# Interleaved block products, adds straight from PSUM, spread weight sums and another DMA order in a fused attention and mixture-of-experts kernel

## The chip, the cores and the metric

The kernel runs on one core of a Trainium2 chip. The metric is the device time of one execution, in microseconds (us), lower is better. Times are medians of several runs; the profile is of one execution.

## The reference

```python
def reference(q, k, v, w_gate, w1, w2):          # q, k, v: 4 x 8 heads x 576 x 64
    scores = q @ k.T / 8                          # per head
    scores = where(0 <= i - j < 64, scores, -1e9) # window of 64
    x = (softmax(scores) @ v)                     # x: 2304 tokens x 512
    P = exp(x @ w_gate - max)                     # 2304 x 8
    for _ in range(8):                            # Sinkhorn
        P /= P.sum(1) + 1e-9
        P /= P.sum(0) + 1e-9
        P *= 2304 / 8
    out = 0
    for e in range(8):                            # w1[e]: 512 x 1024, w2[e]: 1024 x 512
        out += P[:, e:e+1] * (relu(x @ w1[e]) @ w2[e])
    return out                                    # float32, 2304 x 512
```

## The kernel before, in words

Every float32 matrix product is done as three products of rounded parts: each operand is split into a high part (a cast to fp32r) and a low part (the operand minus its high part), and high*high, high*low and low*high are added in PSUM. Most products also go by a seven-product scheme on 2x2 blocks (Strassen-Winograd): a product needs sums of blocks of its operands, and its seven products are added up in three PSUM accumulators, a, b and c (tags qa, qb, qc, two buffers each).

The 18 tiles of 128 tokens are worked on in three passes of six tiles. The program has three stages.

Stage 1 is attention for all 18 tiles, on TensorE, with the first half of expert 0 for them. The tiles of passes 1 and 2 write their x to DRAM (`xd_r`), and the block sums of x, four operations of GpSimd for each pair of tiles (`x_sums`, L293 to L300), are written to `xd_t`. The rows of expert 0's first half go to `yd`.

Stage 2 is pass 0. It has 15 units (u = 0 to 14) of two groups; a group is 256 of the 1024 hidden columns of an expert. `Group.run` (L225) does the seven products of a group (`product`, L203; the matmuls are L209, 128x384 each, six for a product), with ScalarE copies that seed a bank with another (L229, L232, L234), ScalarE relu (L214) and VectorE low parts (L219) and adds (L222). Its hooks `extra(0)` to `extra(3)` issue side work: `even(k)` in the first group, `odd(k)` in the second. Then `mm2` (L257) does six output tiles, each twelve matmuls 128x512 (L268) into a PSUM tile yp, of which there are two buffers, and one VectorE operation that scales and adds it to `acc` (L287; expert 0: L275). Beside this the weights of the next groups are fetched (`fetch1`, `fetch2`: L121, L128), summed on GpSimd for w1 (`sums1`, L138 to L141), split into high and low on ScalarE and GpSimd (`split1`: L156, L158; `split2`: L171, L172), and kept in DRAM for the later passes (`keep1`: w1d, L163). For w2 the four block sums are VectorE's (`sums2`, L182 to L185); they are written to a tile tf, of which there is one, and `keep2` (L191) writes it to w2d. `sums2(s+2)` stands at the end of the first group and `sums2(s+3)` at the end of the second.

Stage 3 is passes 1 and 2. `first(p, i)` (from L875 on) does the seven products of a group i with the kept w1 (L209 again) and makes seven high and low tiles G of its relu (L886, L889, and `part_s` L892 on ScalarE, L893 on GpSimd, for the four block sums sm made at L896 and L924). `second(p, u, o)` (L927 on) does, for a pair o of token tiles, seven products with the two groups of unit u (L940, 128x256, six for a product), four scaled adds to `acc` (`out_add`, L947), two ScalarE copies (p5 L956, u2 L958), the seed copy L953 and two VectorE adds (L963, L966). `split_w2` (L867 on ScalarE, L868 on GpSimd) splits the kept w2 blocks, from a queue `bulk` that is worked off a piece at a time. The order is first(0), first(1), first(2), unit 0, first(3), first(4), unit 1 and so on, where a unit is second for o = 0, 1, 2; each second and each first is issued whole. At a pass's end the finished rows of `acc` go out, and those of the next pass's `yd` come in, in turn (L289 and L290; L993 and L995), and `load_x` reads the next x and its sums.

The order on each engine is the order in which the program is written (manual scheduling), and all DMAs are issued by SyncE in program order; a DMA that has to wait holds up those behind it.

Of the kernel before, what the change touches and what calls it, by code (L numbers as in the profile page):

```python
# [21 lines left out]
def window_attention_sinkhorn_moe(ctx: ExitStack, tc: tile.TileContext, q, k, v, w_gate, w1, w2, out):  # L22
# [46 lines left out]
    xd_t = [dram.tile([P, 4, 2, NB], F32, name=f"xd_t{p}") for p in range(1, NPASS)]  # L69
# [30 lines left out]
    r_tf = Ring("tf", [P, 4, 2 * P], F32, 0, 1)  # L100
# [23 lines left out]
    def fetch2(i):  # L124
        if i < len(groups):
            e, c = groups[i]
# [48 lines left out]
    tsum = {}  # L175

    def sums2(i):
        if i >= len(groups):
            return
        a, t = raw2.pop(i), r_tf.new()  # L180
# [5 lines left out]
        tsum[i] = t  # L186

    def keep2(i):
        if i < len(groups):
            u, g = divmod(i, 2)  # L190
            nc.sync.dma_start(out=w2d[u][:, :, g], in_=tsum.pop(i))  # L191
# [65 lines left out]
    def mm2(u, t):  # L257
# [60 lines left out]
    with tc.manual_schedule():  # L318
        with ExitStack() as p1:
            at_p = p1.enter_context(tc.tile_pool(name="at", bufs=2))  # L320
            ps_h = p1.enter_context(tc.tile_pool(name="ps_h", bufs=3, space=PSUM))
# [28 lines left out]
            def load_qkv(t, names="kqv"):  # L350
                for nm in names:
                    src = {"k": k, "q": q, "v": v}[nm]
                    x = at_p.tile([P, H, D], F32, tag=nm, name=nm, bufs=3 if nm == "v" else 2)
# [13 lines left out]
            def new_kT(t):  # L367
                kT[t] = at_p.tile([P, G, WIN + P], F32, tag="kT", name="kT")
# [102 lines left out]
            def x_parts(j):  # L471
# [4 lines left out]
                for slot, k0, c0 in ((0, 0, 0), (1, 2, 0), (2, 2, P)):  # L476
                    dst = f32(xc[slot]) if pp == 0 else xd_r[pp - 1][:, slot]
                    for a in range(2):
                        nc.sync.dma_start(out=dst[:, a, :, cols], in_=f32(x[:, a, k0:k0 + 2, c0:c0 + P]))
                xt = at_p.tile([P, 4, 2, P], F32, tag="xt", name="xt", bufs=1)  # L480
                x_sums(xt, xr[j], nc.gpsimd)
                if pp:
                    nc.sync.dma_start(out=xd_t[pp - 1][:, :, :, cols], in_=xt)
                    return
# [89 lines left out]
            for nm, src in (("k", k), ("q", q)):  # L574
                raw[nm, 0] = at_p.tile([P, H, D], F32, tag=nm, name=nm, bufs=2)
# [106 lines left out]
        def load_x(p, xt):  # L682

# [368 lines left out]
```

## Time and profile before

| | us |
|---|---|
| median of three runs | 1776.28 |
| lowest and highest | 1768.73 and 1780.81 |
| the profiled execution | 1783.53 |
| its span, first to last instruction | 1781.8 |
| TensorE busy | 1640.1 (92% of the span) |
| GpSimd, VectorE, ScalarE busy | 1002.6, 947.0, 825.2 |
| mean granted TensorE clock | 0.951 |

PE is TensorE (PEld its weight loads), DVE VectorE, ACT ScalarE, POOL GpSimd, SP SyncE. A row of a timeline has start, duration, engine, line, operation, output<-inputs, shapes, how many instructions follow each other (x6), and in brackets how long the engine stood idle before, and for whom. The chain of waits lists start, duration and what was running, followed back from the end. A row of the stretches has length, then busy time and instructions of PE, PEld, DVE, ACT and POOL, the granted clock (1.00 is full), the DMA share and GB/s.

### The profile page before, as it was taken

The page shows a single profiled execution, that of the slowest core. Times are in us where ns is not written, and L with a number is a line of the kernel's source. Part 1 is how long each engine was busy: PE and PEld are TensorE (multiplying, and loading weights), DVE is VectorE, ACT ScalarE, POOL GpSimd, SP SyncE. Part 2 cuts the span into 40 slices and gives each one's busy share as a digit, 9 for nine tenths or more (in the row PEclk, how much of TensorE's full clock was granted, in tenths as well). Part 3 has the DMA queues.
Part 4 walks back from the last instruction along what each step waited for, and adds up shares of the span by engine and source line. Part 5 has one row for each costly group of instructions (what it writes and reads, how often), then busy time and mean ns, then how long its engine had stood idle before and what let it go on. Part 6 is the DMA issues. An engine that isn't in the chain of part 4 may idle for free.

```text
span 1781.8 us, 29339 instructions
## 1 busy us (share of the span) xinstructions
PE 1640.1 (92%) x10875; PEld 1531.1 (86%) x10875; DVE 947.0 (53%) x1742; ACT 825.2 (46%) x1856; POOL 1002.6 (56%) x924
## 2 busy tenths in 40 slices
PE   7999967889989999895899999999979999999998
PEld 6778766778877888785899999999969999999998
DVE  6456446665554445543455555565535555555554
ACT  5556432333332233323455555555534555555553
POOL 6234445645565455615565656565646566665654
PEclk9899988999998999998899999999988999999999
DMA  8675655564445544465555555555763555555551
GB/s 196 145 163 126 169 178 177 204 232 156 177 154 207 221 162 159 161 271 185 176 172 180 185 180 184 182 185 167 259 218 132 164 203 166 206 160 193 177 177 60
DMA packets 210831, 319.26 MB, mean 179 GB/s; under 512 B 68416, under 2 KB 143168, under 8 KB 206848
## 3 DMA queue, kind: packets, MB, share of 16 engines
q1 hardware_dynamic: 210688, 317.39, 54.1%
q8 instruction: 85, 1.39, 0.3%
q14 instruction: 58, 0.48, 0.1%
HBM read 223.89 MB, written 86.51 MB: 174 GB/s over the span
## 4 chain that ended last, share of the span: by engine, by line
PE 62%; DVE 10%; DMA 7%; ACT 2%; POOL 2%; issue 1%; SPq 1%; DVEq 0%; POOLq 0%; ACTq 0%
PE qb L940 12%; PE qb L209 11%; PE yp L268 11%; PE qa L209 8%; PE qc L209 8%; PE qc L940 6%; PE qa L940 6%; DMA w2d<-tf 4%; DVE tf L183 2%; DVE g L219 2%; DMA out_dram<-acc 2%; DVE tf L184 1%; DVE tf L182 1%; ACT g L214 1%; DVE sm L896 1%
## 5 line engine op out<-in xcount | busy, mean ns | idle before, releaser
L868 POOL TENSOR_TENSOR wp<-wr,wp 128x512 fp32r<-128x512 f32 x210 | 279.3, 1342 | 135.5 <-ACT wp L867 86.5
L209 PE MATMUL qb<-xc,w1c 128*128 128x384 f32 x1620 | 329.4, 339 | 14.5 <-ACT qb L229 5.4
L268 PE MATMUL yp<-w2c,g 128*128 128x512 f32 x1080 | 284.5, 425 | 59.1 <-DVE acc L287 37.8
L268 PEld LDWEIGHTS yp<-w2c,g 128*128 128x128 f32 x1080 | 223.2, 209 | 113.4 <-DVE acc L287 42.4
L209 PEld LDWEIGHTS qb<-xc,w1c 128*128 128x128 f32 x1620 | 287.9, 190 | 15.7 <-ACT qb L229 5.8
L940 PE MATMUL qb<-wp,G 128*128 128x256 f32 x1620 | 255.3, 294 | 25.5 <-ACT qb L953 12.8
L940 PEld LDWEIGHTS qb<-wp,G 128*128 128x128 f32 x1620 | 211.7, 191 | 39.7 <-ACT qb L953 21.5
L893 POOL TENSOR_TENSOR G<-sm,G 128x384 fp32r<-128x384 f32 x240 | 241.4, 1040 | 0.0
L209 PE MATMUL qa<-xc,w1c 128*128 128x384 f32 x1080 | 220.5, 340 | 10.2 <-DMA w1c<-w1d 10.2
L209 PE MATMUL qc<-xc,w1c 128*128 128x384 f32 x1080 | 218.2, 337 | 0.0
L924 POOL TENSOR_TENSOR sm<-sm,r 128x384 f32<-128x384 f32 x60 | 61.1, 1018 | 268.3 <-DVE sm L896 206.4
L172 POOL TENSOR_TENSOR w2c<-stg,w2c 128x512 fp32r<-128x512 f32 x60 | 86.0, 1454 | 212.3 <-PE qb L209 202.3
L209 PEld LDWEIGHTS qa<-xc,w1c 128*128 128x128 f32 x1080 | 192.1, 190 | 11.6 <-DMA w1c<-w1d 10.5
L209 PEld LDWEIGHTS qc<-xc,w1c 128*128 128x128 f32 x1080 | 191.7, 189 | 0.0
L940 PE MATMUL qc<-wp,G 128*128 128x256 f32 x1080 | 160.3, 284 | 3.9 <-POOL G L893 3.5
L940 PE MATMUL qa<-wp,G 128*128 128x256 f32 x1080 | 160.4, 285 | 0.0
L222 DVE TENSOR_TENSOR c<-qb,p 128x384 f32<-128x384 f32 x60 | 33.5, 558 | 223.6 <-PE qb L209 223.6
L867 ACT CAST wp<-wr 128x512 fp32r<-128x512 f32 x210 | 127.6, 622 | 49.5 <-DMA wr<-in_moe_w_dram 35.4
L940 PEld LDWEIGHTS qc<-wp,G 128*128 128x128 f32 x1080 | 143.8, 193 | 4.7 <-POOL G L893 3.9
L940 PEld LDWEIGHTS qa<-wp,G 128*128 128x128 f32 x1080 | 146.0, 193 | 0.0
L892 ACT CAST G<-sm 128x384 fp32r<-128x384 f32 x240 | 120.0, 513 | 55.3 <-DVE sm L896 49.1
L947 DVE SCALAR_TENSOR_TENSOR acc<-qa,prob,acc 128x256 f32<-128x256 f32 x90 | 43.6, 484 | 145.0 <-PE qa L940 145.0
(166 smaller groups left out, 2350.0 us busy)
## 6 DMA issues: line engine op xcount, KB each, us to landing
w1c<-w1d SPq DMA_DIRECT2D x180, 512.0 KB, 5.5
w1d<-w1c SPq DMA_DIRECT2D x30, 1792.0 KB, 11.0
stg<-in_moe_w_dram SPq DMA_DIRECT2D x62, 512.0 KB, 5.3
wr<-w2d SPq DMA_DIRECT2D x120, 256.0 KB, 3.0
wr<-in_moe_w_dram SPq DMA_DIRECT2D x90, 256.0 KB, 2.8
w2d<-tf SPq DMA_DIRECT2D x30, 512.0 KB, 5.1
w1c<-w1d SPq DMA_DIRECT2D x60, 256.0 KB, 2.8
xd_r<-xs SPq DMA_DIRECT2D x36, 128.0 KB, 2.5
```

Source lines behind the costliest of these rows:

```text
L172: nc.gpsimd.tensor_tensor(out=w[:, 1], in0=src[:, j], in1=f32(w[:, 0]), op=ALU.subtract)
L183: nc.vector.tensor_tensor(out=t[:, 1], in0=t[:, 0], in1=b22, op=ALU.subtract)
L209: nc.tensor.matmul(bank, lhsT=w[:, ws, a, kk, :], rhs=xc[xs][:, b, kk, :], start=(first and j == 0), stop=(j == 5), skip_group_check=not f ...
L219: nc.vector.scalar_tensor_tensor(out=g[:, 1, :], in0=src, scalar=0.0, in1=f32(g[:, 0, :]), op0=ALU.max, op1=ALU.subtract)
L268: nc.tensor.matmul(yp, lhsT=g[:, a, o:o + P], rhs=w[:, x, :], start=(i == 0), stop=(i == 11))
L867: nc.scalar.copy(out=t[:, :, 0, :], in_=r)
L868: nc.gpsimd.tensor_tensor(out=t[:, :, 1, :], in0=r, in1=f32(t[:, :, 0, :]), op=ALU.subtract)
L892: nc.scalar.copy(out=g[:, 3 + k, 0, :], in_=sm[k])
L893: nc.gpsimd.tensor_tensor(out=g[:, 3 + k, 1, :], in0=sm[k], in1=f32(g[:, 3 + k, 0, :]), op=ALU.subtract)
L924: nc.gpsimd.tensor_tensor(out=sm[2], in0=sm[1], in1=r22, op=ALU.add)
L940: nc.tensor.matmul(bank, lhsT=G7[p, 2 * u + g][:, gp, x, cols], rhs=W[p, u, wp][:, g, y, :], start=(start and j == 0), stop=(j == 5), skip ...
L947: nc.vector.scalar_tensor_tensor(out=at, in0=src, scalar=prob[:, t0 + row, e:e + 1], in1=at, op0=ALU.mult, op1=ALU.add)
```

## The change

What it does, part by part:

1. **w2 sums in stage 2.** tf has two buffers. `sums2` puts its four operations into a list `t_ops`, and `sum_step` issues one of them behind each output tile of `mm2`, one more at the start of each group of the next unit. The sums are those of the groups s+4 and s+5 (before: s+2 and s+3); those of the first four groups are done in the last two units, from four further fetches.
2. **x sums of passes 1 and 2.** Attention writes the raw x to DRAM (`xd_f`). `next_sums` reads it back in stage 2 and does the 24 GpSimd operations there, in units 4 to 6 (pass 2) and 9 to 11 (pass 1). Pass 1's stay in SBUF, so `load_x(1)` reads three blocks rather than seven.
3. **Pools.** The attention tiles of q, k and kT lie at the other side of SBUF, so other tiles are under the ones of stage 2.
4. **Row DMAs.** The in-turn pair L289 and L290 is gone. All six output rows are issued together behind the first three w2 loads of stage 3, and the six loads of `acc` in the first group. At the end of pass 1 they are split likewise. `load_x(2)` is issued earlier, its high and low parts are made inside the last unit.
5. **Stage 3.** `first` and `second` become classes with `step(n)`, one product each. Neighbours are interleaved: each block issues 6, 2, [1 of the next block], 7, 3, [5 of the next block], 4. In `Second` the copies p5 and u2 and the two adds are gone: six `out_add` read PSUM directly. The scaling of `acc` by the first gate column is moved from GpSimd (L980) to VectorE.

The core of the diff:

```diff
-    r_tf = Ring("tf", [P, 4, 2 * P], F32, 0, 1)
+    r_tf = Ring("tf", [P, 4, 2 * P], F32, 0, 2)
...
     def sums2(i):
-        nc.vector.tensor_tensor(out=t[:, 0], in0=b12, in1=b11, op=ALU.subtract)
-        nc.vector.tensor_tensor(out=t[:, 1], in0=t[:, 0], in1=b22, op=ALU.subtract)
-        nc.vector.tensor_tensor(out=t[:, 2], in0=b22, in1=b12, op=ALU.subtract)
-        nc.vector.tensor_tensor(out=t[:, 3], in0=b21, in1=t[:, 1], op=ALU.add)
+        for k, x, y, op in ((0, b12, b11, ALU.subtract), (2, b22, b12, ALU.subtract), (1, t[:, 0], b22, ALU.subtract), (3, b21, t[:, 1], ALU.add)):
+            t_ops.append(lambda k=k, x=x, y=y, op=op: nc.vector.tensor_tensor(out=t[:, k], in0=x, in1=y, op=op))
...
-        if e == E - 1 and not first:
-            nc.sync.dma_start(out=out[tt * P:(tt + 1) * P, :], in_=at)
-            nc.sync.dma_start(out=at, in_=yd[FIRST[1] + t])
...
+                if pp:
+                    nc.sync.dma_start(out=xd_f[pp - 1][jj], in_=xr[j])
+                    return
                 xt = at_p.tile([P, 4, 2, P], F32, tag="xt", name="xt", bufs=1)
                 x_sums(xt, xr[j], nc.gpsimd)
-                if pp:
-                    nc.sync.dma_start(out=xd_t[pp - 1][:, :, :, cols], in_=xt)
-                    return
...
                 for t in range(TP):
+                    if t == 0:
+                        sums2(s + 4)
+                        sums2(s + 5)
                     mm2(u, t)
+                    sum_step(2 if last and t > 3 else 1)
...
-                product(1, a, True)
-                nc.scalar.copy(out=b, in_=a)
-                do_bulk(1)
-                product(5, c, True)
-                nc.scalar.copy(out=p5, in_=c)
-                product(6, b, False)
-                nc.scalar.copy(out=u2, in_=b)
-                do_bulk(2)
-                product(2, a, False)
-                out_add(1, 0, a)
-                product(7, b, False)
-                nc.vector.tensor_tensor(out=c22, in0=b, in1=p5, op=ALU.add)
-                out_add(0, 1, c22)
-                product(3, c, False)
-                nc.vector.tensor_tensor(out=c, in0=c, in1=u2, op=ALU.add)
-                out_add(1, 1, c)
-                product(4, b, False)
-                out_add(0, 0, b)
+                    elif n == 5:
+                        self.product(5, self.c, True)
+                        self.out_add(0, 1, self.c)
+                    elif n == 6:
+                        self.product(6, self.b, False)
+                        self.out_add(1, 1, self.b)
+                    elif n == 2:
+                        self.product(2, self.a, False)
+                        self.out_add(1, 0, self.a)
+                    elif n == 7:
+                        self.product(7, self.b, False)
+                        self.out_add(0, 1, self.b)
+                    elif n == 3:
+                        self.product(3, self.c, False)
+                        self.out_add(1, 1, self.c)
+                    else:
+                        self.product(4, self.b, False)
+                        self.out_add(0, 0, self.b)
...
+            for _ in range(3):
+                load_w2()
+            queue_w2((1, 0), range(7))
+            out_rows(0, range(TP))
...
+                hook(F[0], 6, lambda p=p: acc_rows(p))
...
+                for k, blk in enumerate(flow):
+                    nx = flow[k + 1] if k + 1 < len(flow) else None
+                    for st in (6, 2, -1, 7, 3, -5, 4):
+                        if st > 0:
+                            go(blk, st)
+                        elif nx:
+                            go(nx, -st)
```

Three places show how it moves the instructions. (A number behind a name tells one tile from the next of its kind.)

First, VectorE in stage 2, from the last product of a unit's second group into its output tiles. Before, tf is the one tile of the w2 sums and stg the fetched weights:

```order
L219 SCALAR_TENSOR_TENSOR g_5_5432<-qb,g_5_5432 128x384
L182 TENSOR_TENSOR tf_5436<-stg_5181 128x256
L183 TENSOR_TENSOR tf_5436<-tf_5436,stg_5181 128x256
L184 TENSOR_TENSOR tf_5436<-stg_5181 128x256
L185 TENSOR_TENSOR tf_5436<-stg_5181,tf_5436 128x256
L287 SCALAR_TENSOR_TENSOR acc<-yp_5455,prob,acc 128x512
L287 SCALAR_TENSOR_TENSOR acc<-yp_5470,prob,acc 128x512
```

and now:

```order
L222 SCALAR_TENSOR_TENSOR g_5_5413<-qb,g_5_5413 128x384
L290 SCALAR_TENSOR_TENSOR acc<-yp_5433,prob,acc 128x512
L184 TENSOR_TENSOR tf_5431<-stg_5385 128x256
L290 SCALAR_TENSOR_TENSOR acc<-yp_5448,prob,acc 128x512
L184 TENSOR_TENSOR tf_5431<-stg_5385 128x256
L290 SCALAR_TENSOR_TENSOR acc<-yp_5463,prob,acc 128x512
L184 TENSOR_TENSOR tf_5431<-tf_5431,stg_5385 128x256
```

The four sums that stood ahead of the first add of an output tile now stand singly behind the adds.

Second, the DMA issues of SyncE at the start of stage 3. Before (wr is a w2 block of stage 3, yd the rows for the next pass):

```order
L290 DMA acc<-yd_100 128x512
L289 DMA out_dram<-acc 128x512
L290 DMA acc<-yd_101 128x512
L861 DMA wr_7435<-in_moe_w_dram 128x2x256
L861 DMA wr_7437<-w2d_138 128x512
L861 DMA wr_7439<-w2d_138 128x512
L700 DMA w1c_7513<-w1d_110 128x512
```

and now:

```order
L194 DMA w2d_144<-tf_7338 512x1x256
L194 DMA w2d_144<-tf_7339 512x1x256
L877 DMA wr_7444<-in_moe_w_dram 128x2x256
L877 DMA wr_7446<-w2d_143 128x512
L877 DMA wr_7448<-w2d_143 128x512
L1031 DMA out_dram<-acc 128x512 x6
L877 DMA wr_7468<-in_moe_w_dram 128x2x256
L877 DMA wr_7482<-w2d_143 128x512
L877 DMA wr_7495<-in_moe_w_dram 128x2x256
L1035 DMA acc<-yd_101 128x512
```

The w2 blocks stand ahead of the row DMAs, and behind the last two writes of w2 sums.

Third, stage 3 where a group of first products meets the products of a unit. Here qa, qb and qc are the banks a, b and c. TensorE before, at the end of a first and the start of a second (L940 is the second, x3 for each of its two groups):

```order
L209 MATMUL qc<-xc_86,w1c_13334 128x384 x6
L209 MATMUL qb<-xc_90,w1c_13334 128x384 x6
L940 MATMUL qa<-wp_13415,G_13256 128x256 x3
L940 MATMUL qa<-wp_13415,G_13546 128x256 x3
L940 MATMUL qc<-wp_13434,G_13256 128x256 x3
L940 MATMUL qc<-wp_13434,G_13546 128x256 x3
L940 MATMUL qb<-wp_13439,G_13256 128x256 x3
```

and now (L975 is the second):

```order
L212 MATMUL qc<-xc_86,w1c_8115 128x384 x6
L975 MATMUL qc<-wp_8206,G_8048 128x256 x3
L975 MATMUL qc<-wp_8206,G_8326 128x256 x3
L212 MATMUL qb<-xc_90,w1c_8115 128x384 x6
L975 MATMUL qb<-wp_8240,G_8048 128x256 x3
L975 MATMUL qb<-wp_8240,G_8326 128x256 x3
L975 MATMUL qa<-wp_8252,G_8048 128x256 x3
L975 MATMUL qa<-wp_8252,G_8326 128x256 x3
L975 MATMUL qa<-wp_8185,G_8048 128x256 x3
L975 MATMUL qa<-wp_8185,G_8326 128x256 x3
L975 MATMUL qb<-wp_8273,G_8048 128x256 x3
```

VectorE there, before:

```order
L896 SCALAR_TENSOR_TENSOR sm0_0_8453<-qb_8388,r22_0_8393 128x384
L896 SCALAR_TENSOR_TENSOR sm1_0_8454<-c22_0_8392,sm0_0_8453 128x384
L896 SCALAR_TENSOR_TENSOR sm3_0_8456<-qc_8389,sm1_0_8454 128x384
L889 SCALAR_TENSOR_TENSOR G_0_8386<-qc_8389,G_0_8386 128x384
L947 SCALAR_TENSOR_TENSOR acc_91<-qa_8469,prob_77,acc_91 128x256
L963 TENSOR_TENSOR c22_0_8474<-qb_8470,p5_0_8472 128x256
```

and now:

```order
L981 SCALAR_TENSOR_TENSOR acc_91<-qc_8445,prob_77,acc_91 128x256
L949 SCALAR_TENSOR_TENSOR sm0_0_8461<-qb_8337,r22_0_8406 128x384
L949 SCALAR_TENSOR_TENSOR sm1_0_8462<-c22_0_8426,sm0_0_8461 128x384
L949 SCALAR_TENSOR_TENSOR sm3_0_8464<-qc_8364,sm1_0_8462 128x384
L900 SCALAR_TENSOR_TENSOR G_0_8405<-qc_8364,G_0_8405 128x384
L981 SCALAR_TENSOR_TENSOR acc_91<-qb_8416,prob_77,acc_91 128x256
```

The second's products 5 and 6 now lie around the first's product 4, and the add of its product 6 (qb) stands behind the first's four operations; TensorE's product 7, the last row of its piece, writes the same bank qb again and comes three products after product 4 of the first.

## Rows read from the trace of the kernel before

**Rows 1.** Stretches of core 0: unit 0, units 1 to 13, unit 14, then stage 3.
```profile
230.50:290.50 60.00, 36.35 (x164) 32.35 (x164) 31.75 (x54) 16.63 (x32) 30.53 (x25) 0.80 0.65 223
290.50:770.70 480.20, 436.65 (x2041) 386.70 (x2040) 254.57 (x365) 167.10 (x324) 272.33 (x234) 0.93 0.50 183
770.70:801.60 30.90, 30.90 (x157) 28.06 (x156) 14.45 (x22) 9.99 (x18) 0.00 (x0) 1.00 0.66 255
801.60:870.80 69.20, 43.13 (x254) 42.16 (x253) 21.92 (x42) 24.89 (x55) 39.91 (x34) 0.78 0.52 174
870.80:1274.50 403.70, 402.19 (x2774) 396.46 (x2773) 224.52 (x448) 222.88 (x502) 253.66 (x223) 1.00 0.54 182
1274.50:1354.90 80.40, 62.81 (x380) 60.01 (x379) 37.88 (x67) 32.98 (x73) 45.54 (x39) 0.87 0.61 210
```

**Rows 2.** The chain of waits in one unit of stage 2.
```profile
522.90 5.34 DMA w2d<-tf
...
529.03 2.48 DVE tf L183
...
533.96 13.99 PE yp L268 x48
```

**Rows 3.** Timeline of all engines at the same place.
```profile
528.68 2.55 POOL L158 TENSOR_TENSOR w1c<-ws,w1c 128x1024 fp32r<-128x1024 f32 x1
...
533.96 2.50 PE L268 MATMUL yp<-w2c,g 128*128 128x512 f32 x5 [3.43 <-DVE acc L287]
```

**Rows 4.** Waits of PE: what for, us in total, times, longest.
```profile
PE yp L268 <- DVE acc L287: 37.8, 11, 4.8
```

**Rows 5.** Timeline of PE in unit 0 of stage 2.
```profile
238.21 2.29 PE L209 MATMUL qb<-xc,w1c 128*128 128x384 f32 x6 [5.44 <-ACT qb L229]
...
277.17 4.59 PE L268 MATMUL yp<-w2c,g 128*128 128x512 f32 x12 [18.21 <-DVE acc L275]
```

**Rows 6.** Timeline of PE where stage 3 begins.
```profile
826.38 2.29 PE L209 MATMUL qa<-xc,w1c 128*128 128x384 f32 x6 [10.15 <-DMA w1c<-w1d]
...
849.57 1.65 PE L940 MATMUL qb<-wp,G 128*128 128x256 f32 x6 [12.50 <-ACT qb L953]
```

**Rows 7.** Timeline of all engines there: SyncE's queue and ACT.
```profile
819.65 0.43 SPq L861 DMA_DIRECT2D wr<-in_moe_w_dram  x1
...
822.68 0.62 ACT L867 CAST wp<-wr 128x512 fp32r<-128x512 f32 x1 [9.63 <-DMA wr<-in_moe_w_dram]
```

**Rows 8.** Timeline of PE from pass 1 to pass 2.
```profile
1272.38 1.21 PE L209 MATMUL qc<-xc,w1c 128*128 128x384 f32 x6
1273.42 1.21 PE L209 MATMUL qb<-xc,w1c 128*128 128x384 f32 x6
...
1282.40 0.88 PE L940 MATMUL qa<-wp,G 128*128 128x256 f32 x6
1283.12 0.88 PE L940 MATMUL qc<-wp,G 128*128 128x256 f32 x6
...
1300.75 1.97 PE L209 MATMUL qb<-xc,w1c 128*128 128x384 f32 x6 [4.58 <-ACT qb L899]
...
1309.15 2.29 PE L209 MATMUL qb<-xc,w1c 128*128 128x384 f32 x6 [4.52 <-ACT u L905]
```

**Rows 9.** Timeline of all engines in stage 3, first to second.
```profile
1644.10 0.87 PE L940 MATMUL qa<-wp,G 128*128 128x256 f32 x6
...
1644.36 0.56 DVE L896 SCALAR_TENSOR_TENSOR sm<-qb,r 128x384 f32<-128x384 f32 x1
...
1646.19 0.55 DVE L889 SCALAR_TENSOR_TENSOR G<-qc,G 128x384 fp32r<-128x384 f32 x1
```

**Rows 10.** Groups of DVE instructions: busy us, mean ns, idle before.
```profile
L947 DVE SCALAR_TENSOR_TENSOR acc<-c,prob,acc 128x256 f32<-128x256 f32 x90 | 69.9, 777 | 3.2
L287 DVE SCALAR_TENSOR_TENSOR acc<-yp,prob,acc 128x512 f32<-128x512 f32 x72 | 53.0, 747 | 119.9 <-PE yp L268 119.6
...
L947 DVE SCALAR_TENSOR_TENSOR acc<-qa,prob,acc 128x256 f32<-128x256 f32 x90 | 43.6, 484 | 145.0 <-PE qa L940 145.0
```

More of the change, by code (lines that the diff above doesn't have):

```diff
@@ L841, in window_attention_sinkhorn_moe @@
             W, R, G7 = {}, {}, {}
-            bulk = []
-            todo = set()
+            bulk, urgent = [], []
+            done_s = set()
             def do_bulk(n):
-                while bulk and n > 0:
-                    bulk.pop(0)()
-                    n -= 1
+                for _ in range(n):
+                    if urgent:
+                        urgent.pop(0)()
+                    elif bulk:
+                        bulk.pop(0)()
             ORDER = (0, 3, 4, 1, 5, 2, 6)
@@ L936, in product, with __init__ @@
+            class Second:
+                def __init__(self, p, u, o):
+                    self.p, self.u, self.o = p, u, o
+                    self.e = groups[2 * u][0]
+                    self.nxt = (p, u + 1) if u + 1 < n_units else (p + 1, 0) if p + 1 < NPASS else None
+                def product(self, n, bank, start):
                     gp, wp = PROD[n]
+                    p, u = self.p, self.u
+                    while (p, u, wp) not in W or (p, 2 * u + 1, gp) not in done_s:
+                        do_bulk(1)
+                    cols = slice(self.o * P, (self.o + 1) * P)
@@ L964, in second, with out_add @@
[L964 to L971 removed]
+                def out_add(self, row, h, src):
+                    t = 2 * self.o + row
+                    at = acc[:, t, h * HD:(h + 1) * HD]
+                    nc.vector.scalar_tensor_tensor(out=at, in0=src, scalar=prob[:, FIRST[self.p] + t, self.e:self.e + 1], in1=at, op0=ALU.mult, op1=ALU.add)
@@ new lines, in plan @@
+            def plan():
+                for p in range(1, NPASS):
+                    more = p + 1 < NPASS
+                    n = len(groups)
+                    F = [First(p, i) for i in range(n)]
+                    S = [[Second(p, u, o) for o in range(TP // 2)] for u in range(n_units)]
+                    flow = [F[0]]
+                    for u in range(n_units - 1):
+                        flow += ([F[1], F[2]] if u == 0 else [F[2 * u + 1], F[2 * u + 2]]) + S[u]
+                    flow += [F[n - 1]]
+                    yield p, F, S, flow
@@ new lines, in window_attention_sinkhorn_moe, with out_rows, acc_rows, scale0 @@
+            plans = list(plan())
+            def out_rows(p, rows):
+                for t in rows:
+                    nc.sync.dma_start(out=out[(FIRST[p] + t) * P:(FIRST[p] + t + 1) * P, :], in_=acc[:, t, :])
+            def acc_rows(p):
+                for t in range(TP):
+                    nc.sync.dma_start(out=acc[:, t, :], in_=yd[FIRST[p] + t])
+            def scale0(p, t):
+                nc.vector.tensor_scalar(out=acc[:, t, :], in0=acc[:, t, :], scalar1=prob[:, FIRST[p] + t, 0:1], scalar2=None, op0=ALU.mult)
@@ L1001, in window_attention_sinkhorn_moe, with hook @@
-                for i in range(n):
-                    if p == 1 and i == 1:
-                        queue_w2(1, 0, ORDER)
-                    if i == 2:
-                        for t in range(TP):
-                            scale0(t)
-                    if i == n - 1:
-                        unit(n_units - 2)
-                    first(p, i)
+                nextF = plans[p][1][0] if more else None
+                hooks = {}
+                def hook(blk, step, *fs):
+                    hooks.setdefault((blk, step), []).extend(fs)
@@ L1027 @@
+                a, b, c = last
+                for blk, st in ((a, 1), (b, 1), (a, 2), (b, 2), (a, 5), (b, 5), (a, 6), (b, 6), (a, 7), (b, 7), (a, 3), (b, 3), (a, 4), (c, 1), (b, 4), (c, 5), (c, 6), (c, 2), (nextF, 1), (c, 7), (c, 3), (nextF, 5), (c, 4)):
+                    if blk:
+                        go(blk, st)
+                while bulk and not more:
+                    do_bulk(1)
 _INS = ["q", "k", "v", "moe_w_gate", "moe_w1", "moe_w2"]
```

299 lines of the change are left out of this document (158 added, 141 removed).

## The prediction

> **What bounds the kernel now.** I read the stretches of the whole span first, then the chain of waits inside a stretch, then the timeline where the chain leaves TensorE. The stretches [rows 1] show TensorE as the bound wherever it is fed: unit 14 of stage 2, which has no w2 sums, is 30.90 us with 30.90 busy at clock 1.00; the long stretch of stage 3 is 402.19 busy of 403.70. The other four rows hold the loss: unit 0 (36.35 busy of 60.00, clock 0.80), units 1 to 13 (436.65 of 480.20, clock 0.93), the start of stage 3 (43.13 of 69.20, clock 0.78) and the passage from pass 1 to pass 2 (62.81 of 80.40, clock 0.87). So TensorE loses time twice: it stands, and then works at a lower granted clock.
>
> In the chain of a stage-2 unit [rows 2] the write of the w2 sums to DRAM (5.34) comes before L183 (2.48), and TensorE's 48 matmuls only after that; the timeline [rows 3] puts TensorE's wait at 3.43, for the add L287. That add is short, 0.747 [rows 10]; it is late because the four sums stand ahead of it on VectorE, and they wait until the one tile tf has been written out. All such waits are 37.8 us in 11 places, the longest 4.8 [rows 4]. They are not the whole price: units 1 to 13 take 480.2/13 = 36.94 each, 6.04 over the 30.90 of unit 14, while the mean wait is 37.8/11 = 3.43. The factor from a wait to its price is 6.04/3.43 = 1.76, the rest being the clock (0.93).
>
> **The change part by part.** The sum is made against the profiled execution, 1783.53 (span 1781.8 and 1.73 around it); it is 0.41% above the median 1776.28.
>
> *Units 1 to 13.* The four sums no longer stand ahead of the first add; each stands behind an add, and with two tf tiles none waits for a write that was just issued. The floor of a unit is unit 14. An output tile has (30.90 - 14 x 1.04)/6 = 2.72 us of matmuls (1.04 is the distance of two first products, [rows 8]); VectorE needs 0.75 for the add, and a sum has to fit into 1.97. L183 took 2.48 in the row shown while GpSimd ran 2.55 of L158 [rows 3]. If every sum took that, VectorE would fall (0.75 + 2.48) - 2.72 = 0.51 behind at each tile, so the add of the fourth tile, the last one that gates a matmul here through the two yp buffers, would come at 3 x 0.51 + 0.75 = 2.28 after its matmuls, still under 2.72. So TensorE should not wait. I leave 5 us for the early units, where the Sinkhorn steps share VectorE: 13 x 30.90 + 5 = 406.7, a gain of 73. Bounds: 45 (a wait of 1.2 us with the factor 1.76 left in each unit) and 78 (no loss at all).
>
> The x sums now done in six of these units are four GpSimd operations each; GpSimd is busy 272.33 of 480.20, so it has the room, and their reads are issued two products ahead. I price them at nothing. If the cover goes, the split L158 of the next weights is late by about the 2.55 of one piece, and that in six units would be 6 x 2.55 x 1.76 = 27.
>
> *Unit 0.* TensorE waits 5.44 for a ScalarE copy and 18.21 for the add L275 [rows 5]. The first stood behind a cast whose target overlapped attention tiles that were still being written out; the new pools lay it elsewhere. The second stood behind three blocks of sums, which are gone from there. New is one: the first spread sum reads weights whose fetch is issued late in unit 0, and the next add queues behind it; I put that wait at 5 us, an estimate from the places of the fetch and the add in the order. With 2.5 for the clock: 30.90 + 0.5 + 5 + 2.5 = 38.9 against 60.0, a gain of 21 (17 to 27).
>
> *Unit 14 and the moved sums.* The sums of groups 0 to 3 come into units 13 and 14, with four fetches. VectorE has 14.45 busy of 30.90 in unit 14, so 0, at worst -3.
>
> *Start of stage 3.* Its work is three firsts and a unit: 21 x 1.04 + 21 x 0.72 = 36.9 (0.72 is the distance of two second products, [rows 8]); it takes 69.2, 32.3 too many. Two waits make 22.65 of it: 10.15 for a w1 load and 12.50 for the copy qb [rows 6]. Both come from SyncE: row DMAs in turn hold the first w2 load until 819.65, and ScalarE's cast stands 9.63 for it at the head of its queue [rows 7]. Now three w2 loads go ahead of the rows. Three waits replace the two: the loads stand behind the last write of w2 sums, so ScalarE's cast waits about 3 us more than the load's 3.03 (issue 819.65 to cast 822.68) and a product of the first group about 3.9; the w1 load of the third group stands behind w2 loads that wait for GpSimd's splits, about 3.2; and the first second waits for its fifth split, about 4.8. These are estimates from the order and the durations. Sum 11.9; with the clock I take 18. Gain 14. Bounds: 6 (26 of the excess stays) and 24 (8 stays).
>
> *Stage 3 in its stride.* The long stretch holds 13 units and one first, so a unit is (403.7 - 7.3)/13 = 30.5, against 14 x 1.04 + 21 x 0.72 = 29.7: about 0.8 us a unit are small waits at the joints, which the interleaving takes away. But it makes one. TensorE's second product 7 comes three second products (2.15 us) after the first's product 4, and it writes a bank that VectorE must have added from; that add stands behind four operations of the first, which today run from 1644.36 to 1646.19 + 0.55 = 1646.74 after product 4 ended at 1644.10 [rows 9], that is 2.64 later. With the add's 0.48 [rows 10] and the hand-over the product starts 3.1 to 3.2 after, a wait of about 1.0. Gain and loss cancel: 0, bounds -28 (the wait at twice this) and +22 (no wait).
>
> The adds from SBUF (777 ns) become adds from PSUM (484 ns) [rows 10], six for four adds and two further operations; the scaling by the first gate column is 6 operations a pass more, at most 0.75 each by L287. VectorE has 224.52 busy of 403.70 [rows 1], and none of it but the wait above lies on the path: 0.
>
> [...]
>
> *From pass 1 to pass 2.* The stretch holds a unit, three firsts and a unit: 52.0 of 80.4, an excess of 28.4. Two waits in it are for ScalarE copies, 4.58 and 4.52 [rows 8], behind row DMAs and the splits of the new x. The new order issues x earlier, spreads its splits over the last unit's second block, and puts products of the next first between the last seconds. I leave 3.5: a gain of 25 (12 to 27).
>
> *Attention and end.* 24 GpSimd operations fewer, and a last second whose products 5 to 4 wait on fewer VectorE operations: 2 and 2 (each 0 to 4).
>
> Sum: 73 + 21 + 0 + 14 + 0 + 25 + 4 = 137. 1783.5 - 137 = 1646.5, and by 0.9959 for the median 1640. If the terms deviate independently (roots of the sums of squares of their bounds), they give about 50 up, the 27 of the x sums with them, and 27 down: 1613 to 1690.
>
> **The rivals.**
> (a) *A sum becomes the new wait.* The contended sums of [rows 2, 3] last as long as today and some wait for their weights; TensorE stands as long as now in every unit, and the 73 are lost: 1719.5, for the median 1712. For it: 2.48 is real. Against: the two yp buffers and the order behind the add.
> [...]
> (b) *Stage 3 gains.* The wait at product 7 is hidden, 22 more: 1624.5, median 1618. For it: the estimate is the difference of two small numbers.
> (c) *Slower.* The wait at product 7 is longer than I work out, VectorE being held by a GpSimd operation beside it, and the clock falls in stage 3 as in stage 2, where 3.43 of wait cost 6.04. 28 units x 6.04 = 169 against 137: 1815.5, median 1808. It decides from 137/28/1.76 = 2.8 us a unit. Against: the four operations took 2.38 in [rows 9], so the wait would have to nearly triple.
> (d) *The passages don't improve.* The DMAs in them are as many, and the new order only moves the waits: 39 lost, 1685.5, median 1679.
>
> **How the numbers follow.** Forecast 0.62, (a) 0.07, (b) 0.15, (c) 0.04, (d) 0.12. The likeliest gives 1640. The range takes in (b) and (d): 1606 to 1690; (a) and (c) and the tails, about 2 in 10, are left out. A measurement of this kernel tells about 1% from no change, the runs before being 0.7% apart. Only (c), and an (a) with (d), end at or above 1758: faster 0.94, same 0.02, slower 0.04.
>
> **What would show it.** Right: units 1 to 13 at about 31 us with clock near 1.00 and no wait of TensorE for L290; unit 0 near 39; a start of stage 3 near 55; one wait of 1 us per unit before a second's product 7 (qb), for VectorE's add. Wrong: a wait of TensorE for an add in stage 2, a clock under 1.00 in stage 3's stride, or a passage that still stands 20 us.

## The result and the profile after

The changed kernel takes 1643.62 us (median of four runs, 1642.84 to 1643.96). The ratio to the kernel before, 1774.8 in the same comparison, is 0.926 with an interval of 0.9228 to 0.9293: 7.4% faster. The profiled execution is 1643.92, its span 1642.1; TensorE is busy 1580.5 of it (96%) at a mean granted clock of 0.992.

The forecast of 1640 is met to 0.2%, but not term by term. In the spans of the two profiled executions the gain is 139.7 (1781.8 to 1642.1). In stage 3 the marks are a unit's product 7, which both kernels have once in a unit's first second; the stretch that begins stage 3 runs to the mark of unit 1 (after, one more product lies ahead of a mark, 0.7 us).

| stretch | before | after | gain | forecast |
|---|---|---|---|---|
| attention | 230.5 | 207.6 | 22.9 | 2 |
| unit 0 of stage 2 | 59.9 | 38.3 | 21.6 | 21 |
| units 1 to 13 | 480.3 | 405.2 | 75.1 | 73 |
| unit 14 | 30.8 | 30.9 | -0.1 | 0 |
| start of stage 3 | 87.1 | 78.7 | 8.4 | 14 |
| stride of stage 3, two times 12 units | 732.2 | 739.3 | -7.1 | 0 |
| pass 1 to pass 2 | 118.1 | 102.6 | 15.5 | 25 |
| end | 43.0 | 39.6 | 3.4 | 2 |

The stretches after, with the columns of [rows 1] (attention, unit 0, units 1 to 13, unit 14, start of stage 3, stride, passage):

```profile
0.00:207.64 207.64, 199.95 (x2219) 167.11 (x2220) 126.85 (x276) 124.81 (x344) 91.65 (x124) 0.99 0.73 173
207.64:245.93 38.29, 33.71 (x163) 30.03 (x163) 20.91 (x41) 13.49 (x27) 24.22 (x21) 0.96 0.73 256
245.93:651.10 405.17, 404.52 (x2040) 366.63 (x2039) 229.68 (x368) 167.27 (x324) 289.46 (x258) 1.00 0.65 231
651.10:682.00 30.90, 30.90 (x157) 28.06 (x156) 16.89 (x30) 9.56 (x18) 0.00 (x0) 1.00 0.88 330
682.00:760.65 78.65, 63.06 (x368) 61.42 (x366) 37.66 (x72) 33.73 (x73) 40.15 (x36) 0.89 0.60 205
760.65:1130.59 369.94, 360.25 (x2521) 357.81 (x2521) 200.96 (x409) 180.38 (x385) 225.43 (x205) 1.00 0.54 180
1130.59:1233.17 102.58, 92.82 (x630) 90.98 (x630) 58.30 (x113) 47.69 (x101) 60.21 (x52) 0.98 0.65 228
```

Units 1 to 13 are now 404.52 busy of 405.17 at clock 1.00, where [rows 1] had 436.65 of 480.20 at 0.93. The stride is where TensorE now stands: 360.25 busy of 369.94. TensorE's waits after, which answer to [rows 4], for the whole execution:

```profile
PE qb L975 <- DVE acc L981: 24.8, 29, 1.8
PE qa L212 <- DMA w1c<-w1d: 10.6, 2, 5.7
PE qb L212 <- ACT u L922: 4.8, 2, 3.8
PE qc L739 <- DVE prob L735: 4.6, 1, 4.6
PE qc L975 <- POOL wp L883: 3.2, 1, 3.2
...
PE yp L271 <- DVE acc L290: 0.6, 1, 0.6
```

The 37.8 us of [rows 4] have become 0.6 in one place; a new wait of stage 3 for VectorE's add stands at the top, 29 times. Its place, in the timeline of all engines after, which answers to [rows 9]:

```profile
757.85 0.56 DVE L949 SCALAR_TENSOR_TENSOR sm<-qb,r 128x384 f32<-128x384 f32 x1 [0.41 <-PE qb L212]
...
758.29 1.60 PE L975 MATMUL qa<-wp,G 128*128 128x256 f32 x12
...
759.65 0.55 DVE L900 SCALAR_TENSOR_TENSOR G<-qc,G 128x384 fp32r<-128x384 f32 x1
...
760.12 0.47 DVE L981 SCALAR_TENSOR_TENSOR acc<-qb,prob,acc 128x256 f32<-128x256 f32 x1
...
760.65 0.98 PE L975 MATMUL qb<-wp,G 128*128 128x256 f32 x6 [0.76 <-DVE acc L981]
```

The four operations of the first run from 757.85 to 760.20, and the add of product 6 behind them from 760.12; product 7 begins at 760.65. The profile counts 0.76 of idle time, from the end of the matmuls before. By the distance of the starts it is 0.92: the two products ahead began at 758.29, and two take 1.44 (0.72 each). This is the wait that the prediction put at about 1.0.

### The profile page after: what moved, and what is told of

Its sections match the earlier page's. It is cut to its first block, busy times and chain, and to the rows that moved or that the text cites. A ratio compares the mean times of both kernels' runs of the same rounds, so it can differ in the third digit from the quotient of the medians.

```text
span 1642.1 us, 29136 instructions
## 1 busy us (share of the span) xinstructions
PE 1580.5 (96%) x10875; PEld 1494.1 (91%) x10875; DVE 912.2 (56%) x1754; ACT 768.1 (47%) x1676; POOL 973.8 (59%) x912
## 4 chain that ended last, share of the span: by engine, by line
PE 84%; DVE 8%; DMA 4%; POOL 1%; ACT 1%; issue 1%; SPq 0%; DVEq 0%; POOLq 0%; ACTq 0%
PE qb L212 16%; PE yp L271 13%; PE qa L212 11%; PE qc L212 11%; PE qb L975 11%; PE qc L975 8%; PE qa L975 5%; DVE sm L949 3%; PE yp L556 3%; PE hp L542 3%; PE vp L462 1%; DMA stg<-in_moe_w_dram 1%; DVE G L900 1%; PE sp L412 1%; DMA wr<-w2d 1%
## 5 line engine op out<-in xcount | busy, mean ns | idle before, releaser
L883 POOL TENSOR_TENSOR wp<-wr,wp 128x512 fp32r<-128x512 f32 x210 | 270.3, 1305 | 178.5 <-ACT wp L882 174.5
L212 PE MATMUL qb<-xc,w1c 128*128 128x384 f32 x1620 | 323.0, 337 | 5.2 <-ACT u L922 4.8
L212 PEld LDWEIGHTS qb<-xc,w1c 128*128 128x128 f32 x1620 | 282.5, 189 | 6.2 <-ACT u L922 5.4
L975 PE MATMUL qb<-wp,G 128*128 128x256 f32 x1620 | 232.5, 286 | 24.8 <-DVE acc L981 24.8
L271 PE MATMUL yp<-w2c,g 128*128 128x512 f32 x1080 | 252.1, 392 | 0.6 <-DVE acc L290 0.6
L975 PEld LDWEIGHTS qb<-wp,G 128*128 128x128 f32 x1620 | 214.6, 191 | 30.9 <-DVE acc L981 30.7
L271 PEld LDWEIGHTS yp<-w2c,g 128*128 128x128 f32 x1080 | 202.9, 189 | 42.9 <-DVE acc L290 1.1
L981 DVE SCALAR_TENSOR_TENSOR acc<-qb,prob,acc 128x256 f32<-128x256 f32 x270 | 130.3, 483 | 152.7 <-PE qb L975 152.5
L975 PE MATMUL qc<-wp,G 128*128 128x256 f32 x1080 | 150.2, 284 | 3.3 <-POOL wp L883 3.2
L975 PE MATMUL qa<-wp,G 128*128 128x256 f32 x1080 | 149.4, 283 | 0.5
L975 PEld LDWEIGHTS qc<-wp,G 128*128 128x128 f32 x1080 | 140.4, 193 | 3.7 <-POOL wp L883 3.4
L975 PEld LDWEIGHTS qa<-wp,G 128*128 128x128 f32 x1080 | 139.6, 191 | 1.3 <-DVE G L900 0.7
```

The costliest lines, as they stand in the source:

```text
L212: nc.tensor.matmul(bank, lhsT=w[:, ws, a, kk, :], rhs=xc[xs][:, b, kk, :], start=(first and j == 0), stop=(j == 5), skip_group_check=not f ...
L271: nc.tensor.matmul(yp, lhsT=g[:, a, o:o + P], rhs=w[:, x, :], start=(i == 0), stop=(i == 11))
L883: nc.gpsimd.tensor_tensor(out=t[:, :, 1, :], in0=r, in1=f32(t[:, :, 0, :]), op=ALU.subtract)
L975: nc.tensor.matmul(bank, lhsT=G7[p, 2 * u + g][:, gp, x, cols], rhs=W[p, u, wp][:, g, y, :], start=(start and j == 0), stop=(j == 5), skip ...
L981: nc.vector.scalar_tensor_tensor(out=at, in0=src, scalar=prob[:, FIRST[self.p] + t, self.e:self.e + 1], in1=at, op0=ALU.mult, op1=ALU.add)
```

## The experiments

Runs given as "one execution" were timed once; the others were timed four times and are given with the range of their times and the ratio to the kernel before. Between these versions, differences of up to some 9 us lie within the intervals of the ratios; they rest on the ranges and on the waits in the traces.

**Attention: writes in SyncE's queue or GpSimd's time.** The six writes of x sums are gone from SyncE's queue in attention; writes of the raw x, which wait for no sum, stand in their place. Before, in SyncE's timeline:

```profile
26.57 4.20 SPq L479 DMA_DIRECT2D xd_r<-xs  x6
37.21 0.58 SPq L483 DMA_DIRECT2D xd_t<-xt  x1
37.88 0.62 SPq L355 DMA_DIRECT2D k<-in_k_dram  x1
```

and after:

```profile
26.62 4.71 SPq L480 DMA_DIRECT2D xd_r<-xs  x6
31.42 0.44 SPq L482 DMA_DIRECT2D xd_f<-xr  x1
31.96 0.40 SPq L356 DMA_DIRECT2D k<-in_k_dram  x1
```

The load of k is issued 5.9 us sooner. Two runs tell the queue from the sums. The first puts both back, with a spare DRAM tile `xd_s` for the writes:

```diff
...
                 if pp:
                     nc.sync.dma_start(out=xd_f[pp - 1][jj], in_=xr[j])
+                    xt = at_p.tile([P, 4, 2, P], F32, tag="xt", name="xt", bufs=1)
+                    x_sums(xt, xr[j], nc.gpsimd)
+                    nc.sync.dma_start(out=xd_s[pp - 1][:, :, :, cols], in_=xt)
                     return
```

> The changed kernel with the block sums of x of passes 1 and 2 computed in attention again as well, by 24 GpSimd operations, and written to a spare DRAM tile by six writes (extra work; nothing is left out). Theory A (the six writes stand in SyncE's queue and wait for GpSimd's sums, so the loads of q and k behind them are issued late): attention goes back from 207.6 to about 228 us, TensorE waiting for k and q some 14 us again. Rival B (GpSimd's operations themselves hold attention): the same here. Rival C (the other side of SBUF for q, k and kT made it): it stays near 208.

One execution: 1661.12. Attention ends at 227.6 and TensorE waits 8.3 for k and 5.9 for q again. The second leaves the write out of this:

> The changed kernel with the 24 GpSimd sums in attention again, but without the six writes. Theory A (SyncE's queue): attention stays at 208 to 210 us. Rival B (GpSimd's time): about 220 to 228. Rival C: near 208, as in the run with the writes.

One execution: 1643.32. Attention ends at 208.3, and the waits for k and q are 0.6 and 0.7, with the 24 GpSimd operations in it. So the writes in SyncE's queue hold 19 to 20 of the 22.9 us that attention gained; the cause of the other 3 or so stays open. GpSimd's time costs nothing there. Nor does the side of SBUF: in the next run, without the other side, attention ends at 207.3.

**Unit 0: the pools.** The first run on them moves only the side:

```diff
-            at_r = p1.enter_context(tc.tile_pool(name="at_r", bufs=2, side="right"))
+            at_r = p1.enter_context(tc.tile_pool(name="at_r", bufs=2))
```

> The changed kernel with q, k and kT at the same side of SBUF as the other attention tiles. Theory (ScalarE's first casts of unit 0 overlap attention tiles): unit 0 of stage 2 has a wait of about 5.4 us for the seed copy again and takes about 45 us rather than 38.3; attention stays at 208. Rival (the wait came from something else that is gone): unit 0 stays at 38 to 39. For attention, rival C above expects about 228.

One execution: 1645.81, unit 0 39.7, no such wait. That is near the rival's outcome, but the edit did not undo the part: ScalarE's casts of the first weights come as early as in the changed kernel, the last of them (L172) at 202.57 for 202.94, and do not stand for the write of ys. The run that undoes it puts q, k and kT into the one pool:

```diff
-            at_r = p1.enter_context(tc.tile_pool(name="at_r", bufs=2, side="right"))
+            at_r = at_p
```

> The changed kernel with q, k and kT back in the one pool of the other attention tiles, so that the first w1 tile of the second buffer overlaps them again (the run with one side only did not bring the overlap back: the cast still waited for loads of q and k alone). Theory (the overlap held ScalarE's cast and with it the seed copy): the wait of about 5 us before a product 6 at the start of stage 2 returns, and unit 0 takes 43 to 48 us rather than 38.3. Rival (the overlap costs nothing once the sums and their writes are gone from attention, since what the cast waits for is then done early): unit 0 stays at 38 to 40.

One execution: 1650.59; unit 0 runs from 207.47 to 251.26, 43.8. ScalarE's cast stands for the write of ys, and TensorE for the copy behind it, in the timeline of this run:

```profile
209.64 0.92 ACT L157 CAST w1c<-stg 128x512 fp32r<-128x512 f32 x2 [8.54 <-DMA yd<-ys]
...
213.29 1.31 PE L212 MATMUL qb<-xc,w1c 128*128 128x384 f32 x6 [3.56 <-ACT qb L232]
```

The kernel before has the same cast, and the same releaser, behind the first wait of [rows 5]; its ScalarE timeline:

```profile
234.55 0.92 ACT L156 CAST w1c<-stg 128x512 fp32r<-128x512 f32 x2 [10.41 <-DMA yd<-ys]
```

So the overlap is what that wait was made of. It returns smaller than expected, 3.56 for about 5 (5.44 before), and the separate pool is worth 5.5 us of unit 0. The other 16 us that unit 0 gained were not taken apart by a run of the changed kernel.

**Stage 2: one tf tile or four sums in a block.** The kernel before, with one number changed:

```diff
-    r_tf = Ring("tf", [P, 4, 2 * P], F32, 0, 1)
+    r_tf = Ring("tf", [P, 4, 2 * P], F32, 0, 2)
```

> The kernel before, with two tf tiles rather than one. Theory (four sums ahead of the first add are the stall, and the wait for the write only makes it longer): VectorE's wait for the write, 1.46, goes, TensorE's wait in a unit of stage 2 falls from 3.43 to about 2.0, and units 1 to 13 take about 34.4 each, 447 in all rather than 480. Rival (the single tile is the whole cause): about 31 each, 405 in all. Second rival (the block alone): no change, 480.

One execution: 1741.79, beside 1770.51 for the kernel before on the same chip. Units 1 to 13 run from 281.95 to 727.92, 446.0 in all or 34.3 each, where 34.4 was expected. Waits of TensorE, and two units in its timeline:

```profile
PE yp L268 <- DVE acc L287: 25.1, 11, 3.5
```

```profile
443.25 11.17 PE L268 MATMUL yp<-w2c,g 128*128 128x512 f32 x48 [2.16 <-DVE acc L287]
...
476.65 12.77 PE L268 MATMUL yp<-w2c,g 128*128 128x512 f32 x48 [2.16 <-DVE acc L287]
```

So of the 6.0 us a unit lost, 2.6 hang on the single tile. The other 3.4 stay with two tiles, where most units still have a stall of 2.16 behind the block of sums; the changed kernel, which spreads the sums, has 0.6 us of waits for this add in the whole stage. In unit 0 the two tiles alone bring the wait for L275 from 18.2 to 10.9.

**Stage 3: product 7 behind product 3.** In the first second of each unit two steps are exchanged:

```diff
-                    for st in (6, 2, -1, 7, 3, -5, 4):
+                    for st in (6, 2, -1, 3, 7, -5, 4) if getattr(blk, "o", 1) == 0 else (6, 2, -1, 7, 3, -5, 4):
```

> The changed kernel with products 7 and 3 exchanged in the first second of every unit (order 6, 2, next 1, 3, 7, next 5, 4). Theory A (the 0.76 us wait of every unit is product 7's, for VectorE's add of product 6 behind the four operations of the first): product 7 comes 0.72 later, the wait falls to 0.1 or less in 28 units, the time falls by some 18 to 20 us, to about 1625. Rival B (VectorE is behind in its whole queue and the wait only moves to another product): the wait reappears at product 4 or in the next second, and the time stays within 5 us of 1643.6.

1628.39 (1627.62 to 1628.50), ratio 0.9188 [0.9151, 0.9225]. The wait is gone from the stride; what is left of it in the whole execution:

```profile
PE qb L975 <- DVE acc L981: 2.7, 4, 1.1
```

A unit is 30.18 (the distance of like products in consecutive units) against 30.78: 0.60 saved where 0.72 was hoped for, and 15.2 us in all, short of the 18 to 20 expected. Theory A holds in kind, smaller in size.

**Start of a pass: the w1 load.** The second group of a pass is issued whole:

```diff
-                    for st in (6, 2, -1, 7, 3, -5, 4):
+                    for st in (6, 2, 7, 3, 4, -1, -5) if blk is F[1] else (6, 2, -1, 7, 3, -5, 4):
```

> The changed kernel with the second group of a pass issued whole, so that the third group's product 1 comes three products later. Theory A (the waits of 5.7 and 4.9 us for w1 come from interleaving: the load can start only when the first group is finished, and the third group's product 1 is now due two products after that): these waits fall by about 3.1 us each, to 2.6 and 1.8, and the time by 6 to 10 us. Rival B (the load is late because it stands behind other DMAs in SyncE's queue, and the waits move with the order): the waits stay at 5 and the time at 1643.

1632.39 (1629.90 to 1632.46), ratio 0.9208 [0.9171, 0.9245]: 11.2 less. The third group's first product in the changed kernel:

```profile
705.01 2.26 PE L212 MATMUL qa<-xc,w1c 128*128 128x384 f32 x6 [5.66 <-DMA w1c<-w1d]
...
1184.31 2.26 PE L212 MATMUL qa<-xc,w1c 128*128 128x384 f32 x6 [4.91 <-DMA w1c<-w1d]
```

and in this run:

```profile
706.98 1.33 PE L212 MATMUL qa<-xc,w1c 128*128 128x384 f32 x6 [0.74 <-DMA w1c<-w1d]
...
1177.49 1.32 PE L212 MATMUL qa<-xc,w1c 128*128 128x384 f32 x6 [0.82 <-DMA w1c<-w1d]
```

The outcome is theory A's, and larger: the waits fall by 4.9 and 4.1 where 3.1 was expected, the time by 11.2 where 6 to 10 was. The interleaving asks for the third group's w1 two products after the first group has freed its tile; here five products lie between. But the interleaving does not make the whole wait. In the changed kernel's chain of waits the load has more ahead of it:

```profile
698.44 1.58 POOL wp L883
...
700.04 0.38 SPq L877
...
700.51 4.36 DMA w1c<-w1d
```

The first group's last matmul ends at 697.27 and frees the tile. SyncE issues the w1 load only at 700.51, 3.2 us later, because a w2 load (L877) ahead of it stands until GpSimd's split (L883) is done. Then the load takes 4.36 us. Against these 7.6 us the interleaved order has two products (2.1) to do; the rest is the wait. Issued whole, the second group covers most of that time: in its run the first group's last product starts at 698.62, five products of the second follow it, and the third group starts at 706.98. The rows show the second price too: after the long wait six matmuls take 2.26, after the short one 1.33.

**Stage 3 without interleaving.** Every block whole, the adds from PSUM kept:

```diff
-                    for st in (6, 2, -1, 7, 3, -5, 4):
+                    for st in (6, 2, 7, 3, 4, -1, -5):
...
-                for blk, st in ((a, 1), (b, 1), (a, 2), (b, 2), (a, 5), (b, 5), (a, 6), (b, 6), (a, 7), (b, 7), (a, 3), (b, 3), (a, 4), (c, 1), (b, 4), (c, 5), (c, 6), (c, 2), (nextF, 1), (c, 7), (c, 3), (nextF, 5), (c, 4)):
+                for blk, st in [(x, y) for x in last for y in (1, 5, 6, 2, 7, 3, 4)] + [(nextF, 1), (nextF, 5)]:
```

> The changed kernel with every group and every second of stage 3 issued whole (order 1, 5, 6, 2, 7, 3, 4 and then the next), all else kept, the adds from PSUM too. Theory A (in its stride the interleaving takes away the waits at the joints, 0.8 us a unit, and puts 0.76 in their place): 30.5 to 30.8 a unit as before, and a time within 8 us of 1643.6, with the w1 wait at the start of a pass smaller. Rival B (the interleaving is what makes stage 3 quicker): 31.5 or more a unit, 1665 or more.

1644.45 (1643.12 to 1649.08), ratio 0.9284 [0.9236, 0.9331]: the same time, as theory A has it. But a unit is 31.02, between the two theories, and more than the 30.78 with interleaving and than the 30.50 before; what the stride loses the start of the passes gives back, since the w1 wait is gone. TensorE's weight loads show what they wait for at a second's product 7:

```profile
847.41 0.78 PEld L975 LDWEIGHTS qb<-wp,G 128*128 128x128 f32 x6 [0.29 <-DVE acc L981]
```

The last run puts the second's old operations back into this one:

```diff
                     elif n == 5:
...
                         self.product(5, self.c, True)
-                        self.out_add(0, 1, self.c)
+                        nc.scalar.copy(out=self.p5, in_=self.c)
                     elif n == 6:
...
                         self.product(6, self.b, False)
-                        self.out_add(1, 1, self.b)
+                        nc.scalar.copy(out=self.u2, in_=self.b)
...
                     elif n == 7:
...
                         self.product(7, self.b, False)
-                        self.out_add(0, 1, self.b)
+                        nc.vector.tensor_tensor(out=self.c22, in0=self.b, in1=self.p5, op=ALU.add)
+                        self.out_add(0, 1, self.c22)
```

(and the same for product 3 with u2; the lines that make the tiles p5, u2 and c22 are left out here).

> As the run with every group and second issued whole, and with the second's two copies, two adds and four scaled adds of the kernel before instead of the six adds from PSUM. Theory (the six adds put VectorE between products 6, 7 and 4 of one bank, and that costs more at the joints than the copies did): the unit of stage 3 goes from 31.02 back to 30.50, and the time falls by 12 to 16 us against 1644.45. Rival (the adds from PSUM cost nothing, the unit of 31.02 has another cause, such as the other queue of splits): the unit stays at 31.0 and the time within 4 us.

1633.49 (1632.35 to 1633.92), ratio 0.9222 [0.9161, 0.9283]; a unit is 30.50 again. The theory's unit is met, its total (12 to 16) nearly, with 11.0. So without interleaving the adds from PSUM cost 0.5 us a unit, and with the old second and no interleaving at all the other parts of the change give 1633.5, which is 10 us better than the whole change. About half of the 0.5 lies at product 7 of a unit's first second, which starts 0.97 after product 2 with the adds and 0.71 with the copies; the other half lies in small gaps between matmuls, whose cause stays open. No run interleaves with the copies kept, so what the adds cost in the interleaved order is not shown by itself.

**Start of stage 3: when the splits are queued.**

```diff
-            queue_w2((1, 0), range(7))
             out_rows(0, range(TP))
             first = plans[0][1][0]
             first.step(1)
             first.step(5)
+            queue_w2((1, 0), range(7))
```

> The changed kernel with the splits of the first seven w2 blocks queued behind the first two products of stage 3 rather than ahead of them. Theory A (the wait of 3.84 us for the copy u, at the start of stage 3, is ScalarE standing at the first cast for its w2 block): the wait goes or falls under 1, and the time falls by 3 to 7 us. Rival B (the splits then come later and the first second waits longer for GpSimd, now 3.2): the wait moves there and the time stays within 2 us.

1647.92 (1647.00 to 1648.99), ratio 0.9299 [0.9262, 0.9337]: 4.3 us worse, where 3 to 7 better was theory A. The wait of 3.84 for the copy u is gone from there, but TensorE then stands longer at the next two places, in this run's timeline:

```profile
703.26 2.26 PE L212 MATMUL qa<-xc,w1c 128*128 128x384 f32 x6 [9.22 <-DMA w1c<-w1d]
...
722.62 0.58 PE L975 MATMUL qa<-wp,G 128*128 128x256 f32 x1 [4.34 <-ACT wp L882]
```

The third group starts at 703.26, nearly when it did (705.01): it was the arrival of w1 that counted, not the copy. Rival B in kind, and worse in size.

**Both other orders, and a last fetch moved.** The two diffs of the exchanged products and the whole second group together:

> The changed kernel with both other orders: products 7 and 3 exchanged in the first second of a unit (15.2 us by itself), and the second group of a pass issued whole (11.2 us by itself). Theory (the two waits lie in different stretches): the gains add, 1617 to 1618 us. Rival (they share a wait or a clock drop at the start of a pass): 1622 or more.

1615.37 (1615.12 to 1616.13), ratio 0.9122 [0.9085, 0.9158]. 28.3 less than the changed kernel, where the single gains sum to 26.4: they add. In the chain of waits of the changed kernel the last fetch of w2 in stage 2 is long:

```profile
669.21 12.44 DMA stg<-in_moe_w_dram
```

so the last run of this line issues it ahead of x, with the last sums earlier:

```diff
                 if last:
+                    fetch2(s + 5)
                     load_x(1, (0, 1, 2))
...
-                    sum_step(2 if last and t > 3 else 1)
+                    sum_step((1, 1, 2, 2, 2, 0)[t] if last else 1)
...
```

> As the run with both other orders, and with the last fetch of w2 in stage 2 issued ahead of the next pass's x rather than behind it, its sums finished two output tiles earlier. Theory (the start of stage 3 is late because the last sums wait for that fetch, which takes 12.4 us behind 2.4 MB of x, and the w2 loads of stage 3 stand behind their write): the waits of 4.6 us for the copy u and of 2 to 3 us for the splits fall by some 3 us each, the time by 4 to 10 us against the run with both orders. Rival (the w2 loads then wait for bandwidth behind x and w1): within 2 us of it.

1612.85 (1611.56 to 1613.32), ratio 0.9104 [0.9061, 0.9148]: 2.5 less than the run before it, whose range it does not touch, but under the 4 expected. The wait for the copy u falls from 3.96 to 0.90 and 1.98 and the one for the split stays at 2.7. This is the quickest version of the study, 1.9% under the changed kernel. The row DMAs of part 4 and the place of the x sums in stage 2 were not undone by themselves.

## Why the forecast was right in the sum, point by point

*Units 1 to 13* were right by their own working: one wait of 0.6 behind an add, 31.2 a unit, 405.2 for 406.7. The working for a contended sum was tested too, since sums still meet splits: the longest, 2.54 to 2.62 us, each beside a split of GpSimd (L159, 2.40 to 2.58), take as long as the 2.48 of [rows 3], while the shortest take 0.41. GpSimd and VectorE after:

```profile
460.52 2.40 POOL L159 TENSOR_TENSOR w1c<-ws,w1c 128x1024 fp32r<-128x1024 f32 x1
460.65 2.56 DVE L184 TENSOR_TENSOR tf<-stg,tf 128x256 f32<-128x256 f32 x1
463.13 0.74 DVE L290 SCALAR_TENSOR_TENSOR acc<-yp,prob,acc 128x512 f32<-128x512 f32 x1
```

The add stood behind that sum, and no matmul of the unit waited. So what rival (a) started from, sums as long as before, came in part, and its consequence did not. The run with two tf tiles splits the cause in the sizes expected (34.3 for 34.4).

*Unit 0* was right: 38.3 for 38.9, with one wait left, 4.58, where 5 was put. It lies at the Sinkhorn step's matmul (L739), behind the same queue of VectorE, and the chain of waits has the fetch there (4.25 from 226.67).

*Attention* was the step that failed most: the 2 us for "24 GpSimd operations fewer" priced GpSimd's time and left out the DMA that the step also moves. Its write waited at the head of SyncE's queue for GpSimd's sums, and the k and q loads of the next tiles stood behind it. The profile of before had it: 37.21 and 37.88 in SyncE's rows above. The runs give the writes 19 to 20 of the 22.9.

*Stage 3 in its stride* failed by 7, and the step that failed is "Gain and loss cancel: 0". Its two terms came in their sizes. The wait at product 7 was found where it was said to be, 0.92 late for about 1.0, and product 7's own matmuls lose 0.1 more (0.98 for the 0.88 of others). The joints were 0.8 a unit before (30.50 over 29.7); after, a unit of 30.78 is 1.1 over 29.7, and without the 1.0 at product 7 only about 0.1 is left, so the interleaving does take them away. But 1.0 lost against 0.8 gained is 0.2 a unit and not 0. Measured it is 0.28 a unit (30.78 for 30.50), in the 24 units of the table 6.7 of the 7.1 us.

The adds from PSUM, put at 0 off the path, are not free in the whole order: 31.02 with them, 30.50 with the copies. There VectorE's add is the releaser of a product in the same bank (the PEld row above). It is not the adds' duration: from PSUM they took 483 ns on the mean after and 484 before, and those from SBUF 777 before [rows 10]. That the loss is one of order, an add standing behind other work of VectorE, fits the rows and is not shown for all of it.

*The passages* gained 8.4 and 15.5 for 14 and 25. The waits for ScalarE's first cast and for the fifth split were named and came (3.84 for 3.9, 3.19 for 4.8). The w1 wait was given 3.2 at the start of stage 3 and was 5.66. The reason given, w2 loads ahead of it that wait for GpSimd's splits, came and costs the 3.2 (697.27 to 700.51 above). What it names nothing for is the load's own 4.36 us, with only two products (2.1) of the interleaved order to cover the whole. In the passage to pass 2, where none was forecast, the wait was 4.91: the tile is free at 1177.33, the load is issued at 1179.14 behind the last loads of `acc` rows, and takes 5.04.

*Rival (c)* did not come. Waits of 0.76 us, one in each unit of stage 3, left the granted clock at 1.00 (stride rows above), so at this size they cost nothing in clock; what waits near 3 us would have cost there, no run shows.

The sum came out by luck: 21 us of unforeseen gain in attention met 21 us of missing gain in stage 3 (20.2 for 41). In the working of the range, the "27 down" comes to 26 from the bounds given; nothing hangs on it.

## What to carry to other kernels

When a step is moved, follow each DMA that it issues through its queue: a write that waits for a computation holds up every load behind it, and here that was worth some 20 us where the computation cost nothing. Where two streams are interleaved, look for the buffer whose time for a refill the interleaving has shortened (w1 here), and for the operation that now stands between two products of one bank; exchanging two steps gave back 15 us. A change of several parts is worth undoing part by part even when it is faster: here interleaving and adds from PSUM together were a loss of 10 us beside the old second issued whole (1643.6 for 1633.5), and with two of the orders changed a gain of 18 (1615.4). Two terms of a sum that nearly cancel still leave their difference, times the number of units.

## What was not expected of the hardware

In the kernel before with two tf tiles, the same wait of 2.16 us before 48 matmuls was followed by 11.17 us in some units and 12.77 in others, in turn for several units: that the granted clock makes the difference is not shown for the single units (its mean was 0.97 from 300 to 700). In the kernel before, the 48 matmuls behind the wait of 3.43 [rows 3] took 13.99 at a mean granted clock of 0.79 (533.96 to 547.95), and from 548 to 564 it was 1.00. In the changed kernel waits of 0.76, one in each 30.8 us, left it at 1.00, and a wait of 5.66 was followed by six matmuls in 2.26 rather than 1.20, at a granted clock of 0.50 (705.01 to 707.07).
